# Two pairs of attention layers on one core: softmax sums, numerators, features and loads moved between engines, in a new written order

## The chip, the cores and the metric

The kernel runs on one core of a Trainium2 chip. The metric is the device time of one execution in microseconds. The kernel before took 480.94 us, the median of three runs (480.47 to 482.35). Engines are named as the profile names them: PE (TensorE), PEld (its weight loads), DVE (VectorE), ACT (ScalarE), POOL (GpSimd) and SP (SyncE, which here only issues transfers).

## The reference, cut to what matters

2,048 tokens of 512 features pass through a layer A, a layer B, and then both again with the same weights. Each layer is `x = x + layer(layernorm(x))`, with 32 heads of 16 features.

```python
# layer A, for each of 4 segments of 512 tokens
p = softmax(qs @ ks.T * scale + mask)              # causal, inside the segment
a_dot = p @ vs
a_mem = (phi(qs) @ M) / (phi(qs) @ z + 1e-6)       # phi(t) = t + 1 if t > 0 else exp(t)
o = g * a_mem + (1 - g) * a_dot                    # g = sigmoid(beta), one per head
M, z = M + phi(ks).T @ vs, z + phi(ks).sum()
# layer B, over all 2048 tokens
phi_k = concat(softmax(k @ w), softmax(-(k @ w)))  # 16 features each; phi_q alike
kv, z = phi_k.T @ v, phi_k.sum()
o = (phi_q @ kv) / (phi_q @ z + 1e-6)
# both: the heads are joined and multiplied by wo
```

## The kernel before

Tokens lie on the partitions in 16 tiles of 128; four tiles make a segment. The whole of `X` (bf16) and all weights stay in SBUF. Nothing loops at run time: `build` records every operation of the two pairs of layers in a graph, and `place` reads one order for all of them, the engine of each and the buffer of each tile from a packed table, `ORDER`. Each engine then runs its own list strictly in that order and waits on semaphores; a late instruction holds whatever stands behind it on its engine. PSUM is four tiles `D0` to `D3` of 128 x 1024 f32, shared by everything that PE writes.

The steps, by the functions that make them:

- `setup` loads inputs and weights on the queues of SP, ACT and POOL, and builds the gate from `beta`. The four token tiles of the first segment are loaded one by one, in turn on SP and ACT. `1 - g` is multiplied into layer A's value weights (four multiplications on POOL), `exp(beta)` into the mask `GAm` of the memory.
- `ln` normalises a tile: statistics, a root on POOL (on ACT for the first segment), and `xn` on DVE; with `flex` it may be on DVE or ACT.
- `a_proj` projects keys and queries of layer A into one PSUM tile. `Kev` and `Qev` copy the two halves to SBUF, `phi` reads the same PSUM half again for its exponential (`phexp`), and `Km` masks the keys per head into `KM`. Then come the values and the memory `M`.
- `a_att` is the causal attention: scores on PE, exponentials on ACT (`exp`, `expf`, `expd`, 1024, 896 and 768 elements per partition), weighted values on PE, the normalisation on DVE (`rden`, `pvn`). The sum of each softmax comes from a column of ones beside the values.
- `b_keys` takes four token tiles: exponentials of both signs on ACT, their sums over 16 features on DVE (`Zred`), reciprocals on DVE (`rZ`, line 389), values times reciprocals (`Vt`), and the product with the values, added up in `KV32`. After the last tile of a layer, `Rkv` and `Rz` are the masked results.
- `b_query` takes the four tiles of a segment: exponentials (`qexp`), sums (`Zq`, `zln`, `zs`), and for each tile a numerator `N` on PE. ACT copies it to SBUF in bf16 (`Nev`, line 351), DVE multiplies it by the weights (`nmul`, line 1043) and adds the two halves (`nadd`, line 1049). A DMA transpose or PE turns the result, and `out_proj` multiplies by `wo` and adds the residual.

Layer B's queries can begin when all keys of the layer are summed. In the order, the queries of the first layer B run beside the projections and the attention of the second layer A; the queries of the last layer B stand alone at the end.

Of the kernel before, what the change touches and what calls it, by code (L numbers as in the profile page):

```python
# [16 lines left out]
D = 512  # L17
H = 32
# [279 lines left out]
class Kernel:  # L298
# [151 lines left out]
    def setup(self):  # L450
# [19 lines left out]
        for t in range(4):  # L470
            ldx(t, 1, "act" if t % 2 else "sp")
        for h in range(2):
            for k in ("k", "q"):
                load(lambda k=k, h=h: [(self.WA[k][:, :, h * 256:(h + 1) * 256],
                                        inp["A_w" + k][:, h * 256:(h + 1) * 256].rearrange("(dt p) o -> p dt o", p=128))],
                     256, [R("WA", k, h)])
        load(lambda: [(self.beta_sb[:], inp["A_beta"].partition_broadcast(128))], 8, [R("beta")], "pool")
        load(lambda: [(self.wphi_st[:], inp["B_w_phi"].rearrange("(g hl) d j -> (hl d) g j", g=NG))], 60, [R("wphi")], "pool")
        ldw(lambda: self.WA["v"], inp["A_wv"], R("WA", "v"))
# [33 lines left out]
        for hf in range(2):  # L513
# [6 lines left out]
        self.act(lambda: gt[:, 0, :], lambda: self.beta_sb[:], ACT.Exp, 32, [R("beta")], [R("gt")], psum=False)  # L520
        v(lambda e: e.tensor_scalar(gt[:, 1, :], gt[:, 0, :], 1.0, None, op0=ALU.add), 100, [R("gt")], [R("gt1")])
        v(lambda e: e.reciprocal(gt[:, 2, :], gt[:, 1, :]), 270, [R("gt1")], [R("gt2")])
        v(lambda e: e.tensor_tensor(self.GAm[:, :, :, 0:16], gt[:, 0, :, None].to_broadcast([128, H, 16]).rearrange("p (g h) c -> p g h c", g=NG),
                                    self.H8[:, None, :, None].to_broadcast([128, NG, 8, 16]), ALU.mult), 620,
          [R("gt"), R("H8")], [R("GAm")], label="gates")
        v(lambda e: e.tensor_copy(self.GAm[:, :, :, 16], self.H8[:, None, :].to_broadcast([128, NG, 8])), 100,
          [R("H8")], [R("GAm")], label="gates")

        for dt in range(4):
            fn = lambda e, dt=dt: e.tensor_tensor(self.WA["v"][:, dt, :].rearrange("p (h d) -> p h d", h=H),  # L530
                                                  self.WA["v"][:, dt, :].rearrange("p (h d) -> p h d", h=H),
                                                  gt[:, 2, :, None].to_broadcast([128, H, DH]), ALU.mult)
            self.g.op({"dve": (602.0, fn), "pool": (1100.0, fn)}, [R("gt2"), R("WA", "v")], [R("WAv", dt)], label="gate")
# [95 lines left out]
    def phi(self, ps, dst, src=None, c=0):  # L629
# [28 lines left out]
    def a_proj(self, L, s):  # L658
# [7 lines left out]
        for g in range(NG):  # L666
# [11 lines left out]
            for sl in range(4):  # L678
# [3 lines left out]
                self.g.op({"dve": (262.0, fn)}, [KT, R("m4")], [KM[sl]], label="Km", port=True)  # L682
            st["KM"].append(KM)
            if pk:
                PK = self.T(self.p1, "PhK")
                self.phi(ps, pk, KT)
# [8 lines left out]
            if PQ:  # L695
                self.phi(ps, PQ, QT, 512)
                st["PhQ"].append(PQ)
        wv = lambda dt: self.WA["v"][:, dt, :].rearrange("p (k a e) -> p a k e", k=8, a=2)
        for t2 in (0, 2):
            ps = self.T(self.pD, "gen")  # L700
            self.tproj(ps, wv, [R("WAv", i) for i in range(4)], (t2, t2 + 1), lambda tt, dt: xT.t[:, dt, tt * 128:(tt + 1) * 128],
# [10 lines left out]
        if s < 3:  # L712
            for hp in range(2):
# [8 lines left out]
                if s == 0:  # L722
                    self.v(lambda e, pv=pv, g2=g2: e.tensor_copy(self.MS32[:, g2], pv()), 350, [ps[0]], [R("MS32", hp)], label="Macc")
# [178 lines left out]
    def kv_add(self, ps, q, first, last):  # L902
# [5 lines left out]
        if first:  # L908
            v(lambda e: e.tensor_copy(dst(), src()), 65 + 136 * n / 0.96, [ps[0]], [R("KV32", q)], label="KVacc")
# [12 lines left out]
    def b_keys(self, L, c, parts):  # L922
# [4 lines left out]
        for part in parts:  # L927
            Es, Vts = {}, {}
            units = [part[i:i + 2] for i in range(0, len(part), 2)]
            for u in units:  # L930
# [9 lines left out]
                for sgn in range(2):  # L940
# [46 lines left out]
    def b_query(self, L, c, store):  # L987
# [21 lines left out]
        zr = [ZQ[(gp, sgn)] for gp in range(2) for sgn in range(2)]  # L1009
        AB = self.T(self.pS, "AB")  # L1010
# [5 lines left out]
        self.act(lambda: u(0), lambda: zv(1, 1), ACT.Ln, 128, zr, [t1[0]], label="zln")  # L1016
# [41 lines left out]
    def build(self):  # L1058
# [5 lines left out]
        def lnA(L, s):  # L1064
            self.xA[(L, s)] = self.T(self.pX, "xA")
            for t in range(s * 4, s * 4 + 4):
                self.ln(t, self.xA[(L, s)], flex=(L == 1), pe=("xA", L, t) in PE_T, root="act" if L == 0 and s == 0 else "pool")

        for L in range(2):
            if L == 0:  # L1070
                lnA(0, 0)
                gate = self.xnop[3]
                for o in list(self.pV.init.values()) + list(self.pE.init.values()) + list(self.pF.init.values()):
                    o.deps.add(gate)
# [36 lines left out]
MASKED = {(0, 0)}  # L1111
N_XT, N_KM, N_K1, N_K2, N_VT, N_SM, N_QT, N_PE, N_PF = 5, 6, 16, 19, 5, 6, 6, 2, 3
PVW = 320
VSP = 1
VCOP = set()
# [7 lines left out]
COPIED = {(L, t) for L in range(2) for t in range(16)}  # L1123
# [6 lines left out]
c-rlH1Jo>AvgVG6?W~{2wr$(CZQHhO+qP}nwr!s?nRQOzzV~+bboadJS@YI<Syh?28DD%6Uu4x<m4sDhRakr$oh4>fSv6Lj)nGMQEmoV=VRczOR-ZLs4Ot`Bm^EQdS  # L1130
u@t0wO}n-E7qE|VQpDE)}D1>ahPUtSqv7F#bUsSAuGxpmX8%<FIaw7hFxO?SV2~tC1ZtHSyqmfXC)Y8oGB()5R1$#%g$c194sfx#Y(aYEH}H(Ua@HGHA}#5u$wGB%g
73|BCHfk&Pub2EDy`eDzX0T4okuAvPA3=OUNFxH|!p}&z`WSEE7x3(y(+aEz8QXu*}S`4D12B#X7P9tP>l^I<sM{AM3%Mu`x`tFzg`<W+Ci3i@*l4p=>Z4!n(7REFS
B^#<Fp2Jev$tU<#YfrotRH4Q8>ftQQ->y0M;Y8tcvGvK1^PRe*}Hh^=J(VF0XR17Qst1m&PStYzz1A2t+*v(;<~o5v=xg={2CMe|u-rZ6i_U<=r7_LfCqKDLi-VCz{
Vc90!lp)4#L1`>)vaVP|ZK|v8H3h&q`HWA)44WW>Vjb_<MV*oB@009sNCc$9X$TqPLY%?1I2wzzyC;_FR6qJFIP!{GwW|#*%U?)_Ds!$24z-Sl=W5B`}W*`g(0$>)X
21{9W$W7tkJ45`)rn1j$6wHRKFdg>59GC&wU@uI7nXnKR!7P}_Vzca!hX}T?PwX2D#NjXk#=|aH#&$z?%0bIn5QfF+EEo+EPG&(6g5l6&c;vVb7QlSigfo}}GueKq3
FBZZ+l;lKE^K3AAw5OF?QAS8hG19%KUia^4M|xB+QIfRAJl_{&;;s0bJ&21papEihR_I_LNjOytzZ>2fYs0jT0?yZU=dj$+s|r1C`QC=OkiS23n?HSBmoX>p&hh`43
G*A!6rDwj<LhA88$$AILwZ-l#mp5vy8A2mcbE-0L$Shtb>TK0@lMy=m2Y=BW!^akQy8m5DDTybchSlARfekn9vDwLR2O(9P?o;2oI4V4J?IIEC(<+f@|R@ZiNGIg6+
eDupdvtI_wFt;UtR>ogoTzfv9kV^@0R&lpVnBa2(d-L2Qfd@EB}^Q*auRL2t-NU7-(jgS?c9l0#qE$-2WX)*cUG2Rw{5u_yMzX4o9pU@hzc{oo9QKyBQ^*5WHnjMuO
wzQz`K9b01(Y=vF14X(mS*bT2>WK4>wFg>ouD3}4SVoZ#O@$nAy!QR*%??Mke3!SkqcEOI=4?E!&JO{Bb8pgn=7#q`IW{QI;Fgf<e0eBvg;WfAb*Wn&KfUUR#Ct@|+
iIZ>}4#n!Y9cy4dx&f)_CZwTTFc2@oFuZ}ga4+7%J$MuI!C1@>xA78OhLl(UcH=nA1>-R{49A3c1@b_2%!CgiBj$yiGyzB8WSoM7aR^Su(Kro{;TRl=CvX%V$5VI)Z  # L1140
^KoXjx#VnrN)_<mhQu2cm$d8EE|NgurB7J0(6?4#B+EDU%+X+i&yCyy@Xfr2F~JnEQ&AiB^JZtcmXeBTD*t%aW=leIhc;J&?UT#b?`M*#8NmHD`N?K3vclOK7of=1}
ot+{DhzJDSW`^_z|<<MY=>;F&jRIXHWnW;5#UUrLipL#Def13Sw@2g5U5vzQYgj9uLzI`Us!l6I`Y%^c4@%V|;|8=nFo@Lo|R!(?I$TBj^X@z#qsc50=A{$gnVG$0A
q-mtZbjid8WYj->r`fI8Aq8bqCl^J6ra1TRQqXe<??64aRr(>yFfJ*gL!q=__v`q41zPhS8z@vktBhSPBxO5^D?4WYc455ED>Bq~mmsWhFW6V!#y&?%DqI&~$*Z_s=
!MP;ZPmB*KKp3c!Ly25VL9qLV2*)m*?D{uiW#0zwn&eC4GM@WmX8118?M0Arl&7fN}lO7S{_vrymqlW}skdGeI6M9MkQ~`U?V$6?c*h)-?3urnurCHR67Se2bOU-Br
y`!bnm)cNsT1NA!5ze8x)EL`RJ8FW9XgR&6c@#>E={c>W6%>Zv&<hGnffPh7sXYagq$#9Glc80#nwp}eHDq~B^6^^a@Bkj3!chaNO%16mX>NEq8pH?lVE&PUcp#5J<
*5pNqN+5N)>3zRMsYEO99l>3=>vVH_4I`*Q3Z-bm8l|Cqlna)s?!FlK^tiZAId}c6#kul&{SRzr}6sujSBPWya@kFvv>pCPN6&uk4&ZcY+i;J<x!|SAI6LE3OqUu=V
# [83 lines left out]
```

## Time and profile before

| what | value |
|---|---|
| median of three runs | 480.94 us (480.47 to 482.35) |
| the profiled execution | 477.48 us |
| its span in the profile | 475.8 us |
| granted clock of PE, mean | 0.989 |
| read from memory, written | 6.32 MB, 2.10 MB |

The profile is of one execution, which was faster than the three timed ones. In the parts below, busy time is the time in which an engine had an instruction in its pipe; in a group's row stand the busy time of the group, the mean duration of one instruction in ns, and the idle time of the engine ahead of it with what ended it. Line 351 is the helper `act` and line 326 the helper `mm`, so rows there are told apart by tiles and shapes. `p`, `pS`, `pT`, `pX` are pools of SBUF buffers, `D` is PSUM.

### The profile page before, as it was taken

The page shows a single profiled execution, that of the slowest core. Times are in us where ns is not written, and L with a number is a line of the kernel's source. Part 1 is how long each engine was busy: PE and PEld are TensorE (multiplying, and loading weights), DVE is VectorE, ACT ScalarE, POOL GpSimd, SP SyncE. Part 2 cuts the span into 40 slices and gives each one's busy share as a digit, 9 for nine tenths or more (in the row PEclk, how much of TensorE's full clock was granted, in tenths as well). Part 3 has the DMA queues.
Part 4 walks back from the last instruction along what each step waited for, and adds up shares of the span by engine and source line. Part 5 has one row for each costly group of instructions (what it writes and reads, how often), then busy time and mean ns, then how long its engine had stood idle before and what let it go on. Part 6 is the DMA issues. An engine that isn't in the chain of part 4 may idle for free.

```text
span 475.8 us, 25262 instructions
## 1 busy us (share of the span) xinstructions
PE 451.6 (95%) x11582; PEld 299.1 (63%) x11582; DVE 435.3 (91%) x968; ACT 424.4 (89%) x560; POOL 61.0 (13%) x145
## 2 busy tenths in 40 slices
PE   8898999999999999998999999999999999999996
PEld 4356665757776676656556667576677666666553
DVE  6998999999899989988999999999999887998883
ACT  3598999999999997488999999999999999676892
POOL 4702020200011011100230031020011020110000
PEclk9999999999999999998999999999999999999799
DMA  8844353350243221200235544632105504100256
GB/s 228 210 111 96 65 88 48 61 92 4 60 83 48 26 37 26 41 2 4 47 68 82 73 73 48 98 60 38 25 4 81 61 15 69 28 12 3 47 100 193
DMA packets 89451, 30.37 MB, mean 64 GB/s; under 512 B 76000, under 2 KB 89344, under 8 KB 89344
## 3 DMA queue, kind: packets, MB, share of 16 engines
q1 hardware_dynamic: 88992, 28.46, 33.0%
q8 instruction: 91, 1.49, 1.3%
q10 hardware_dynamic: 288, 0.26, 0.2%
q0 software_dynamic: 64, 0.02, 0.2%
q14 instruction: 16, 0.13, 0.1%
HBM read 6.32 MB, written 2.10 MB: 18 GB/s over the span
## 4 chain that ended last, share of the span: by engine, by line
PE 62%; ACT 27%; DVE 5%; issue 2%; DMA 2%; SPq 1%; POOL 0%
PE D L341 39%; PE D L326 21%; ACT p L351 14%; ACT pF L351 8%; ACT pE L351 4%; PE D L649 2%; DVE pQ L679 1%; DMA pX<-p 1%; DMA p<-p 1%; SPq L364 1%; DVE p L1043 1%; DVE stats L577 1%; ACT pS L351 1%; PE D L378 1%; PE D L867 1%
## 5 line engine op out<-in xcount | busy, mean ns | idle before, releaser
L351 ACT ACTIVATE p<-D 128x1024 bf16<-128x1024 f32 (+1 forms) x276 | 251.5, 964 | 26.4 <-PE D L341 15.9
L351 ACT ACTIVATE pF<-D 128x896 bf16<-128x896 f32 x128 | 117.7, 942 | 2.1 <-PE D L326 1.7
L326 PE MATMUL D<-pK,pQ 64*128 64x256 bf16 (+3 forms) x1536 | 113.5, 243 | 5.8 <-DVE pQ L679 2.0
L326 PEld LDWEIGHTS D<-pK,pQ 64*128 64x128 bf16 x1536 | 55.3, 94 | 44.1 <-ACT p L351 6.7
L326 PE MATMUL D<-pV,pF 64*128 64x34 bf16 x1024 | 76.0, 176 | 1.8 <-ACT pE L351 0.5
L326 PE MATMUL D<-pW,pF 64*128 64x34 bf16 x1024 | 73.2, 176 | 0.3 <-issue 0.3
L341 PE MATMUL D<-pX,WA_k 64*128 64x512 bf16 x256 | 64.7, 376 | 0.8 <-DVE pX L360 0.7
L341 PE MATMUL D<-pX,WA_q 64*128 64x512 bf16 x256 | 64.7, 377 | 0.1
L585 POOL TENSOR_SCALAR rstd<-mv 128x1 f32<-128x1 f32 x60 | 16.5, 285 | 354.5 <-DVE mv L578 354.5
L326 PEld LDWEIGHTS D<-pV,pF 64*128 64x128 bf16 x1024 | 56.9, 93 | 4.3 <-issue 1.1
L326 PEld LDWEIGHTS D<-pW,pF 64*128 64x128 bf16 x1024 | 52.5, 93 | 1.6 <-issue 0.8
L351 ACT ACTIVATE pE<-D 128x768 bf16<-128x768 f32 x64 | 52.8, 835 | 0.2
L326 PE MATMUL D<-pV,p 64*128 64x34 bf16 x1024 | 52.1, 175 | 0.1
L326 PE MATMUL D<-pW,p 64*128 64x34 bf16 x1024 | 51.0, 176 | 0.0
L326 PEld LDWEIGHTS D<-pV,p 64*128 64x128 bf16 x1024 | 46.8, 93 | 2.5 <-ACT p L351 0.4
L326 PEld LDWEIGHTS D<-pW,p 64*128 64x128 bf16 x1024 | 45.1, 93 | 1.7
L326 PE MATMUL D<-tri,two 64*128 64x128 bf16 (+1 forms) x384 | 46.1, 234 | 0.0
L326 PE MATMUL D<-pV,pE 64*128 64x34 bf16 x512 | 45.2, 175 | 0.2 <-issue 0.2
L577 DVE BATCH_NORM_STATS2 stats<-X 128x6 f32<-128x512 bf16 x64 | 42.9, 681 | 1.5 <-DMA X<-in_A_x_dram 1.3
L679 DVE TENSOR_SCALAR pQ<-p,m 128x512 bf16<-128x512 bf16 x128 | 43.8, 363 | 0.0
L326 PE MATMUL D<-pW,pE 64*128 64x34 bf16 x512 | 42.6, 175 | 0.0
L945 DVE TENSOR_REDUCE pS<-p 128x64 f32<-128x1024 bf16 (+1 forms) x36 | 38.6, 1085 | 1.4 <-ACT p L351 1.3
(119 smaller groups left out, 1001.0 us busy)
## 6 DMA issues: line engine op xcount, KB each, us to landing
pW<-pV SPq DMA_DIRECT2D x16, 136.0 KB, 2.8
out_dram<-X SPq DMA_DIRECT2D x7, 256.0 KB, 2.8
X<-in_A_x_dram SPq DMA_DIRECT2D x3, 512.0 KB, 4.6
pX<-in_B_wqkv_dram SPq DMA_DIRECT2D x3, 512.0 KB, 4.9
p<-p SPq DMA_TRANSPOSE x76, 2.6
pX<-p SPq DMA_TRANSPOSE x54, 3.3
WA_k<-in_A_wk_dram SPq DMA_DIRECT2D x2, 256.0 KB, 6.7
WA_q<-in_A_wq_dram SPq DMA_DIRECT2D x2, 256.0 KB, 7.1
```

The costliest lines, as they stand in the source:

```text
L326: ins = e.matmul(out_ap, lhsT, rhs, start=st, stop=sp, tile_position=(basep(lhsT), basep(out_ap)))
L341: ins = e.matmul(out_ap, lhsT[64 * hf:64 * hf + 64], rhs[64 * hf:64 * hf + 64], start=k == 0 and i == 0, stop=k == 1 and i == len(lists[hf ...
L351: return self.g.op({"act": (dur, lambda e: e.activation(out_ap(), in_ap(), func, scale=scale))}, reads, writes, opens, label=label)
L364: return self.g.op({"sp": (1200.0, lambda e: [e.dma_start(out_ap(), in_ap(), transpose=True)])}, reads, writes, opens, kind="d", lat=1450. ...
L378: ins = e.transpose(pb()[:, k * 128:(k + 1) * 128], src()[:, k * 128:(k + 1) * 128], self.ident[:])
L577: v(lambda e: e.bn_stats(self.stats[:, t, :], self.X[:, t, :]), 602, [R("X", t)], [R("st", t)], label="bn")
L585: v(lambda e: e.tensor_scalar(rs, self.mv[:, t, 1:2], LN_EPS, None, op0=ALU.add), 170, [R("mv", t)], [R("rstd", t)], eng="pool", label="rstd")
L649: ins = e.matmul(D.t[c0:, r0 * 8:r0 * 8 + n], r[:, c0:], ones(r, n), start=True, stop=True, tile_position=(r0, c0))
L679: fn = lambda e, KM=KM, KT=KT, sl=sl: e.tensor_scalar(KM.t[:, :, sl % 2, :, 64 * (sl // 2):64 * (sl // 2) + 64], KT.t[:].rearrange("p (j h ...
L867: ins = e.matmul(tp.t[:, k * 128:(k + 1) * 128], pair.t[:, (k // 2) * 512 + sgn * 256 + (k % 2) * 128:(k // 2) * 512 + sgn * 256 + (k % 2) ...
L945: fn = lambda e, sgn=sgn, eo=eo, Z=Z, n=n: e.tensor_reduce(Z.t[:, 0:64 * n].rearrange("p (k s h) -> p k s h", k=n, s=2)[:, :, sgn, :], eo( ...
L1043: v(lambda e, Ns=Ns, Tm=Tm, w=w, shape=shape: e.tensor_tensor(shape(Tm.t[:]), shape(Ns.t[:]), w(), ALU.mult), 600, [Ns, AB[0], AB[1]], [Tm ...
```

## The change

It has six parts and a new table.

- Layer B's keys: where two tiles are taken together, the sums' reciprocals are made on ACT as exp(-ln(z)), one logarithm for the two tiles and one exponential for each, where DVE made them in one operation per tile.
- Layer B's queries: `COPIED` is empty, so `nmul` reads the numerator from PSUM and the copy `Nev` is gone.
- Layer A's features: `phi` reads the copied keys or queries from SBUF, and not the PSUM tile.
- The gate: `1 - g` is no longer multiplied into the value weights. The column beside the values holds `1 + exp(beta)` where it held ones, so that each softmax sum carries the gate; the mask of the memory changes to match. `beta` is loaded as one row and spread by a small matmul.
- Loads: the first segment comes in two loads of two tiles, one on ACT's queue and one on SP's; one half of the query weights moves to ACT's queue; `beta` moves from POOL's queue to SP's, and the load of `w_phi` waits for the fourth `xn`.
- Some operations may now be put on DVE or ACT (`xn` of two more segments, the first copies of `M` and `KV32`, `Km` in two segments), and the table decides.
- The table `ORDER` is new in whole: engine, place and buffer of each operation. In it five `xn` and four of the copies `ote` are on ACT that were on DVE, and no `Km` is.

```diff
-        for t in range(4):
-            ldx(t, 1, "act" if t % 2 else "sp")
+        ldx(0, 2, "act")
+        ldx(2, 2)
...
-                     256, [R("WA", k, h)])
-        load(lambda: [(self.beta_sb[:], inp["A_beta"].partition_broadcast(128))], 8, [R("beta")], "pool")
+                     256, [R("WA", k, h)], "act" if q else "sp")
...
+        load(lambda: [(self.beta_sb[0:1, :], inp["A_beta"][None, :])], 8, [R("beta0")])
...
-        for dt in range(4):
-            fn = lambda e, dt=dt: e.tensor_tensor(self.WA["v"][:, dt, :].rearrange("p (h d) -> p h d", h=H),
...
-            self.pV.init[i] = two(lambda e, tv=tv: e.memset(tv[:, :, :, 16:17], 1.0), 560.0, 190.0)
+            self.pV.init[i] = self.v(lambda e, tv=tv: e.tensor_copy(tv[:, :, :, 16:17], gt[:, 1, :][:, None, :, None].to_broadcast([128, 4, H, 1])), 200.0,
...
-        self.act(lambda: e_.t[:], lambda: ps.t[:, c:c + 512], ACT.Exp, 512, [ps[c]], [e_], label="phexp")
+        self.act(lambda: e_.t[:], lambda: src.t[:], ACT.Exp, 512, [src], [e_], psum=False, label="phexp")
...
+                Zr = [Z[0], Z[1]]
+                if n == 2:
+                    self.act(lambda Z=Z: Z.t[:, 0:128], lambda Z=Z: Z.t[:, 0:128], ACT.Ln, 128, Zr, Zr, psum=False, label="zkl")
                 for k, tt in enumerate(u):
                     Vt = Vts[tt] = self.T(self.pT, "Vt")
+                    if n == 2:
+                        self.act(lambda Vt=Vt: Vt.t[:, :, :, 16, :], lambda Z=Z, k=k: Z.t[:, k * 64:k * 64 + 64].rearrange("p (s g h) -> p s g h", s=2, g=NG), ACT.Exp, 64,
+                                 Zr, [Vt[("z", 0)], Vt[("z", 1)]], scale=-1.0, psum=False, label="zkl")
+                        continue
...
-                self.ln(t, self.xA[(L, s)], flex=(L == 1), pe=("xA", L, t) in PE_T, root="act" if L == 0 and s == 0 else "pool")
+                self.ln(t, self.xA[(L, s)], flex=(L == 1 or s < 2), pe=("xA", L, t) in PE_T, root="act" if L == 0 and s == 0 else "pool")
...
-COPIED = {(L, t) for L in range(2) for t in range(16)}
+COPIED = set()
...
```

More of the change, by code (lines that the diff above doesn't have):

```diff
@@ L700, in a_proj @@
             ps = self.T(self.pD, "gen")
[L701 removed]
+            self.tproj(ps, wv, [R("WA", "v")], (t2, t2 + 1), lambda tt, dt: xT.t[:, dt, tt * 128:(tt + 1) * 128],
                        [xT[t2], xT[t2 + 1]], opens=[VT] if t2 == 0 else [], label="V")
@@ L1009, in b_query @@
         zr = [ZQ[(gp, sgn)] for gp in range(2) for sgn in range(2)]
+        inps = (L, c) not in ZCOP
+        if not inps:
+            ZS = self.T(self.p2, "T")
+            two = lambda x: x.rearrange("p (a x) -> p a x", a=2)
+            self.evac(lambda: two(ZS.t[:].bitcast(F32)), lambda ZQ=ZQ: two(ZQ.t[:])[:, :, 0:256], 512, zr, [ZS], label="Zev")
+            zr = [ZS]
+            zv = lambda s, k: two(ZS.t[:].bitcast(F32)).rearrange("p a (s k x) -> p a s k x", s=2, k=2)[:, :, s, k, :]
         AB = self.T(self.pS, "AB")
@@ L1072, in build @@
                 gate = self.xnop[3]
+                self.loads[self.late].deps.add(gate)
                 for o in list(self.pV.init.values()) + list(self.pE.init.values()) + list(self.pF.init.values()):
@@ L1114 @@
 VSP = 1
+ZCOP = set()
 VCOP = set()
```

164 lines of the change are left out of this document (88 added, 76 removed).

## The prediction

> **What bounds the kernel now.** I read the page's busy lines first, then the busy time of each engine by stage, then the waits, then the groups of instructions of the whole run and of the last stage.
>
> ```profile
> PE 451.6 (95%) x11582; PEld 299.1 (63%) x11582; DVE 435.3 (91%) x968; ACT 424.4 (89%) x560; POOL 61.0 (13%) x145
> PE 62%; ACT 27%; DVE 5%; issue 2%; DMA 2%; SPq 1%; POOL 0%
> ```
>
> ```profile
> 0.00:11.40 11.40, 9.56 (x99) 4.83 (x100) 7.13 (x23) 4.26 (x12) 4.27 (x19) 1.00 0.88 224
> 40.00:185.00 145.00, 140.89 (x4191) 99.81 (x4189) 135.69 (x292) 141.92 (x179) 15.84 (x38) 1.00 0.32 53
> 185.00:214.84 29.84, 29.77 (x593) 18.93 (x587) 26.98 (x51) 19.84 (x24) 3.22 (x8) 1.00 0.09 18
> 214.84:260.00 45.16, 42.75 (x878) 25.51 (x872) 42.63 (x112) 43.58 (x67) 8.64 (x16) 0.96 0.30 53
> 260.00:400.00 140.00, 135.43 (x4046) 95.23 (x4044) 132.46 (x306) 137.55 (x176) 16.07 (x40) 1.00 0.36 53
> 400.00:438.85 38.85, 37.98 (x792) 24.01 (x788) 36.31 (x61) 28.37 (x34) 3.17 (x8) 1.00 0.09 19
> 438.85:475.80 36.95, 30.71 (x646) 17.61 (x644) 25.70 (x55) 26.40 (x43) 0.00 (x0) 0.90 0.45 110
> ```
>
> The columns are the stretch, its length, then busy PE, weight load, DVE, ACT and POOL. No engine has much room, and the tightest one changes. In the attention stretches (40 to 185 and 260 to 400) ACT is busy 97.9% and 98.2%; in the key stretches that end each layer's attention (185 to 214.84, 400 to 438.85) PE is (99.8%, 97.8%) and ACT has 10 us to spare; in the last stretch, layer 1's queries alone, all three have some room. The last wait of an attention stretch is PE held up by exponentials that have not yet read its PSUM tile:
>
> ```profile
> PEld D L326 <- ACT p L351: 10.6, 33, 0.9
> PEld D L326 <- ACT pF L351: 7.5, 28, 0.6
> ```
>
> **The change part by part.** Prices come from groups of the whole run (count | busy, mean ns):
>
> ```profile
> L1043 DVE TENSOR_TENSOR p<-p,pS 128x1024 bf16<-128x1024 bf16 x32 | 21.5, 686 | 2.0 <-ACT p L351 1.7
> L973 DVE TENSOR_TENSOR pT<-D,pT 128x1024 bf16<-128x1024 f32 x28 | 33.3, 1213 | 2.0 <-PE D L341 1.7
> L389 DVE RECIPROCAL pT<-pS 128x64 bf16<-128x64 f32 x28 | 14.4, 533 | 0.1
> L598 DVE TENSOR_SCALAR p<-X,mv,rstd 128x512 bf16<-128x512 bf16 x48 | 18.8, 402 | 0.9 <-POOL rstd L587 0.7
> L360 DVE CAST p<-D 128x512 bf16<-128x512 f32 x27 | 18.5, 685 | 2.2 <-PE D L867 1.7 <-PE D L341 0.4
> L351 ACT ACTIVATE p<-D 128x1024 bf16<-128x1024 f32 x220 | 222.5, 1049 | 23.9 <-PE D L341 14.5 <-PE D L326 7.7
> L351 ACT ACTIVATE p<-D 128x512 bf16<-128x512 f32 x56 | 32.9, 634 | 2.5 <-PE D L341 1.4 <-DVE p L360 1.0
> L351 ACT ACTIVATE pS<-pS 128x128 f32<-128x128 f32 x22 | 6.9, 326 | 0.2
> L351 ACT ACTIVATE pS<-D 128x128 f32<-128x128 f32 x8 | 2.3, 284 | 0.0
> L583 ACT ACTIVATE rstd<-rstd 128x1 f32<-128x1 f32 x4 | 0.7, 199 | 0.1
> L359 ACT ACTIVATE p<-D 128x512 bf16<-128x512 f32 x15 | 9.2, 611 | 5.5 <-PE D L341 5.2 <-PE D L867 0.4
> L592 DVE SCALAR_TENSOR_TENSOR nb<-mv,rstd 128x1 f32<-128x1 f32 x16 | 2.4, 152 | 0.3 <-POOL rstd L587 0.2
> ```
>
> Numerators from PSUM: 32 ACT copies of 128x1024 go, at 222.5/220 = 1.01 us that is 32.4 us of ACT. The 32 multiplications now read f32 from PSUM. That form is not in the trace; line 973 has the nearest (PSUM numerators times a broadcast bf16), 33.3/28 = 1.19 us against 21.5/32 = 0.67 for the SBUF form, so +0.52 each and +16.6 us of DVE. The low bound is 0.67 (no gain of width is lost), and nothing suggests above 1.22.
>
> Key sums on ACT: 28 reciprocals go, 14.4 us of DVE. In come 14 logarithms over 128 elements (0.31) and 28 exponentials over 64 that are not shown, between 0.20 (one element) and 0.33 (128); I take 0.27. That is 4.3 + 7.6 = 11.9 us of ACT (10 to 13.6). It also makes a chain DVE, ACT, DVE out of one that stayed on DVE.
>
> Features from SBUF: 48 exponentials over 512 read SBUF; rows of 128 elements differ by 326 - 284 = 42 ns, so +2.0 us of ACT (0 to 4). In return a projection's PSUM tile is free after one reader.
>
> Moved by the new order, counted from the built program: five normalisations of 0.40 us go from DVE to ACT (not shown there; some 0.65 by the 512-wide row, 3.2 us), eight small statistics of 0.15 us are added on DVE, and four transposed outputs go from DVE (0.69) to ACT (0.6). Sum for ACT: -32.4 + 11.9 + 2.0 + 3.2 + 2.4 and -0.6 for one value copy that leaves = -13.5 us. Sum for DVE: +16.6 - 14.4 - 2.0 + 1.2 - 2.7 + 0.7 + 0.4 of set-up = -0.2 us. PE's instructions stay but for one 32-column matmul. So the change is a trade, and what counts is where each half falls.
>
> Counting both programs' lists between the same events (last attention exponential, last key-value mask) at these prices gives, after minus before: attention of layer 0, ACT +4.8, DVE 0, PE +1.7; keys behind it, ACT -1.8, DVE -4.0, PE -4.2 (a query projection, four small sum products and half a value projection moved out); queries of layer 0 with attention of layer 1, ACT -2.2, DVE -1.1, PE +1.8; keys of layer 1, ACT -1.9, DVE -1.2, PE -0.9; the last stage, ACT -11.4, DVE +7.6, PE +1.7.
>
> Taken by the tightest engine of each stretch: +4 (ACT at 97.9%; 0 to +5), -4 (PE at 99.8%; -4.2 to 0), -1 (ACT; -5 to +2), -1 (PE; -1 to 0).
>
> The last stage has rows of its own:
>
> ```profile
> 437.56 1.28 DVE L915 TENSOR_TENSOR Rkv<-KV,H 128x512 bf16<-128x512 f32 x2
> 439.49 0.29 DVE L1018 TENSOR_TENSOR pS<-pS,D 128x128 f32<-128x128 f32 x1 [0.65 <-ACT pS L351]
> 439.81 0.29 DVE L1019 TENSOR_TENSOR pS<-pS,D 128x128 f32<-128x128 f32 x1
> 464.45 0.69 DVE L1043 TENSOR_TENSOR p<-p,pS 128x1024 bf16<-128x1024 bf16 x1 [0.51 <-ACT p L351]
> 470.10 1.22 DVE L898 TENSOR_TENSOR X<-X,D 128x1024 bf16<-128x1024 bf16 x1 [2.24 <-PE D L341]
> 471.44 0.60 ACT L359 ACTIVATE X<-D 128x512 bf16<-128x512 f32 x1 [1.79 <-PE D L341]
> L1049 DVE TENSOR_TENSOR p<-p 128x512 bf16<-128x512 bf16 x14 | 5.8, 421 | 0.2
> L898 DVE TENSOR_TENSOR X<-X,D 128x1024 bf16<-128x1024 bf16 x4 | 4.8, 1216 | 2.4 <-PE D L341 2.2
> ```
>
> Before, DVE's last numerator ends at 464.45 + 0.69 = 465.14, 26.3 us after the masks (437.56 + 1.28 = 438.84). In the new list DVE does, between those two events, 20 small sums at the 0.32 that lies between starts here (6.4), 16 multiplications of 1.19 (19.0), 13 additions of 0.41 (5.4) and a residual of 1.2: 32.0 us, to which come the 0.65 before the first and about 1 us of other gaps. The last numerator then ends near 33.6, 7.3 later. Of the 475.8 - 465.14 = 10.7 us behind it some 2.3 come back: two of its three residual additions of 1.2 us now lie before it, and the rest (transpose, copy, projection, evacuation, store) hangs on the last tile as before. So the stage costs +5 (+2 to +8): it is bound by DVE, and ACT's freed 11 us stand idle there.
>
> The start: two tokens' tiles per load, one load on each queue, and a weight half on ACT's queue.
>
> ```profile
> X<-in_A_x_dram ACTq DMA_DIRECT2D x2, 128.0 KB, 2.8
> X<-in_A_x_dram SPq DMA_DIRECT2D x2, 128.0 KB, 4.4
> WA_q<-in_A_wq_dram SPq DMA_DIRECT2D x2, 256.0 KB, 7.1
> 2.29 0.44 SPq L457 DMA_DIRECT2D WA_k<-in_A_wk_dram  x1
> 6.66 0.29 ACT L581 ACTIVATE rstd<-mv,epsln 128x1 f32<-128x1 f32 x1 [3.67 <-DVE mv L578]
> 11.40 0.37 PE L341 MATMUL D<-pX,WA_k 64*128 64x512 bf16 x1 [0.72 <-DVE pX L360]
> ```
>
> The same 128 KB landed in 2.8 us from ACT's queue and 4.4 from SP's with its backlog, so the load that leads to PE's first projection at 11.40 could come 1 us sooner. Against that the query weights are now issued behind ACT's first root (6.66 + 0.29) and, at 2.8 to 7.1 us, land at 9.8 to 14. The gate's load leaves POOL's queue for SP's, ahead of the key weights: one issue, 0.44 us. The load that stays on POOL now waits for the fourth normalisation; behind it stand only roots of later tiles. I count 0 (-1 to +3). The Trainium skill's page "DMA: Bandwidth & Descriptors", section "Issuing engines are not separate DMA queues", says that loads from several engines share the same 16 DMA engines and save only issue time; the rows above show a gain beyond that, and by the page the start would be no better than 0.
>
> The gate in the sums' column takes four weight multiplications off POOL (busy 13%) and nothing off the path; their cover is that the value projection comes later.
>
> Sum: 0 + 4 - 4 - 1 - 1 + 5 = +3 us. The profiled execution took 477.48 us, 475.8 of it span; it becomes 480.5. The runs' median of 480.94 lies 3.46 above the profiled one, so the forecast is 484.0.
>
> **The rivals.** (1) Faster. Projections free their PSUM tile after one reader, and ACT's copies are gone from the queries of layer 0, where ACT is busy 43.58 of 45.16 us. If the 18 us of weight loads held up by exponentials shrink by a quarter, the attention terms become +2 and -5 instead of +4 and -1, the start -1 and the tail, with DVE's gaps filled, +3: -1 + 2 - 4 - 5 - 1 + 3 = -6, 478. It decides once ACT's stalls there fall by over 3 us. Against it: ACT's work before the last stage falls by 1 us only. (2) Slower by a new wait: ACT's logarithm of the key sums waits for DVE's reduction with the exponentials of attention queued behind it. The crossing ACT to DVE cost 0.65 at 439.49; 14 crossings there, on an ACT that has no slack, are 9 us, of which I let half stand: 488.5. For it: DVE is busy 93% and more of the attention stretches, so its reductions can run late. It decides if the reductions come less than 0.65 before their logarithm. (3) No change to be told: the trade evens out, 481. (4) The tail's clock. The last stage was granted 0.90; with DVE as its bound PE has longer gaps. At 0.5 its 30.71 busy us would be 55, 13 more than the some 42 us of my tail: 497. The Trainium skill's "TensorE: Matmul & The Clock Gate", section "HAM oscillation — how this bites in real kernels", says that PE gaps above about 3.4 us halve the clock; no gap so long shows in the rows here.
>
> **How the numbers follow.** Forecast 0.40, rival 1 0.25, rival 2 0.15, rival 3 0.17, rival 4 0.03. What can be told from no change here is 0.5%, 2.4 us. The forecast's own range is 479 to 490, since the bounds of its terms do not all fall on one side; a tenth of the total lies in it within 2.4 us and 0.03 below. Faster: 0.22 of rival 1 and 0.03, 0.25. Same: 0.10, 0.03 of rival 1, 0.15 of rival 3: 0.28. Slower: the rest, 0.47. The range is 476 to 490: it leaves out the far half of rival 1, rival 4 and part of rival 2.
>
> **What would show it.** Right: numerators near 1.2 us each; DVE busy about 33 us behind the last mask with ACT below 18, that stage some 42 us long, and the key stretch of layer 0 shorter by 4 while its attention is longer by as much. Wrong: a tail no longer than 38 us, numerators under 1 us, or an attention stretch that shrinks. Rival 2 would show as ACT waiting for DVE's reduction in the waits.

## The result: 2.3 us longer, and the profile after

| | median | range | ratio to before |
|---|---|---|---|
| before | 481.29 us | 479.13 to 485.20 (20 runs) | 1 |
| after | 483.63 us | 479.83 to 489.26 (20 runs) | 1.0048 (95%: 1.0025 to 1.0071) |

The changed kernel is 2.3 us longer, 1.2 to 3.4 by the interval: told apart from zero, and about half a per cent. One run of after, 489.26 us, fell in a slower state and is left out of the ratio. The forecast was 484.0. The profiled execution of after took 479.83 us, the shortest of its twenty, with 478.0 us of span against 475.8 before; its stages therefore show 2.2 us of the difference, and its start, as will be seen, is luckier than most.

The page after, busy time and the chain that ended last:

```profile
PE 453.6 (95%) x11583; PEld 296.6 (62%) x11583; DVE 433.1 (91%) x944; ACT 410.4 (86%) x578; POOL 51.6 (11%) x138
PE 58%; ACT 18%; DVE 18%; DMA 4%; issue 2%; POOL 1%; SPq 0%; DVEq 0%
```

ACT lost 14.0 us (forecast 13.5) and DVE 2.2 (forecast 0.2). The chain moved from ACT (27% to 18%) to DVE (5% to 18%) and PE stayed its largest part.

The same chain of stages, cut at the same events in both kernels (first projection, last attention exponential of layer 0, its last key-value mask, the two for layer 1, the end). Columns as in the prediction. Before:

```profile
0.00:11.40 11.40, 9.56 (x99) 4.83 (x100) 7.13 (x23) 4.26 (x12) 4.27 (x19) 1.00 0.88 224
11.40:185.84 174.44, 166.28 (x4604) 113.65 (x4606) 164.90 (x364) 165.19 (x210) 25.58 (x56) 1.00 0.39 73
185.84:214.76 28.92, 28.85 (x538) 18.21 (x536) 26.16 (x50) 18.93 (x24) 3.22 (x8) 1.00 0.09 18
214.76:408.13 193.37, 186.39 (x5151) 126.23 (x5145) 181.58 (x426) 189.02 (x252) 25.40 (x58) 0.99 0.34 52
408.13:438.84 30.71, 29.84 (x576) 18.60 (x568) 29.81 (x52) 20.55 (x24) 2.49 (x7) 1.00 0.07 15
438.84:475.80 36.96, 30.72 (x646) 17.61 (x644) 25.71 (x56) 26.41 (x43) 0.00 (x0) 0.90 0.45 110
```

After, with the part of the last stage up to the last numerator as a row more:

```profile
0.00:11.91 11.91, 10.12 (x99) 4.88 (x100) 6.59 (x26) 4.81 (x13) 1.75 (x14) 1.00 0.90 248
11.91:185.10 173.19, 166.33 (x4606) 112.76 (x4608) 160.81 (x363) 167.32 (x225) 20.69 (x53) 1.00 0.42 71
185.10:212.42 27.32, 27.13 (x514) 17.07 (x512) 24.64 (x47) 17.79 (x27) 3.22 (x8) 1.00 0.09 17
212.42:407.43 195.01, 188.27 (x5172) 126.15 (x5166) 180.19 (x411) 185.27 (x257) 22.76 (x57) 1.00 0.32 52
407.43:437.34 29.91, 29.28 (x580) 18.30 (x573) 28.70 (x47) 19.80 (x31) 3.13 (x8) 1.00 0.07 15
437.34:478.00 40.66, 32.43 (x654) 17.41 (x646) 32.21 (x54) 15.37 (x29) 0.00 (x0) 0.90 0.47 100
437.34:468.20 30.86, 27.01 (x586) 14.30 (x580) 28.74 (x52) 13.57 (x26) 0.00 (x0) 0.89 0.39 58
```

| stage | forecast | after less before in the two profiles |
|---|---|---|
| start | 0 | +0.5 |
| attention of layer 0 | +4 | -1.2 |
| keys of layer 0 | -4 | -1.6 |
| queries of layer 0, attention of layer 1 | -1 | +1.6 |
| keys of layer 1 | -1 | -0.8 |
| last stage | +5 | +3.7 |
| sum | +3 | +2.2 |

The last stage is the only large term, and DVE, 25.7 us busy there before, has 32.2 now while ACT falls from 26.4 to 15.4. A single profile moves by itself, though: the last mask of layer 1 ended between 437.3 and 442.4 us in the profiles of after, a_load4, hybrid, a_tail_quick and a_l0_quick, which differ little ahead of it. So the terms of 1 or 2 us need the runs below.

The last stage itself is steadier. From the last mask to the end it took 36.96, 36.93, 36.55 and 36.35 us in the four profiles of kernels that have before's last stage unaltered (before, b_act_load, b_phi_sbuf, b_zk_act), and 40.66, 39.73, 39.88 and 39.81 us in the four that have after's (after, a_rz_dve, a_load4, a_l0_quick): 3.3 us more on average. In the second four the granted clock of the stage was 0.90, 0.98, 0.93 and 0.93: at 0.98 the stage was 0.1 us shorter than at 0.93, so it is not PE's clock that sets its length.

The groups that carry the prices, after:

```profile
L1068 DVE TENSOR_TENSOR p<-D,pS 128x1024 bf16<-128x1024 f32 x32 | 38.3, 1218 | 1.6 <-PE D L326 1.4
L351 ACT ACTIVATE pT<-pS 128x64 bf16<-128x64 f32 x28 | 6.6, 266 | 0.1
L351 ACT ACTIVATE p<-pK 128x512 bf16<-128x512 bf16 x24 | 15.1, 640 | 0.0
L351 ACT ACTIVATE p<-p 128x512 bf16<-128x512 bf16 x24 | 14.9, 636 | 0.1
L598 ACT ACTIVATE p<-X,nb,rstd 128x512 bf16<-128x512 bf16 x5 | 3.9, 809 | 0.3 <-DVE nb L595 0.2
```

A numerator from PSUM took 38.3/32 = 1.20 us (1.19 in the sum), a key exponential 0.27 (as estimated), the features 15.1 + 14.9 + 4.7 for the eight that still read PSUM = 34.7 against 32.9 (+1.8; 2.0 in the sum), a normalisation on ACT 0.8 (0.65 in the sum). The prices were near, though the features' came out by another way: their instructions were no longer than before (640 and 636 ns against a mean of 634), so the 42 ns more for each did not show, and only the busy time rose. What the prices did to the time was not right, stage by stage.

### The profile page after: what moved, and what is told of

Its sections match the earlier page's. It is cut to its first block, busy times and chain, and to the rows that moved or that the text cites. A ratio compares the mean times of both kernels' runs of the same rounds, so it can differ in the third digit from the quotient of the medians.

```text
span 478.0 us, 25222 instructions
## 1 busy us (share of the span) xinstructions
PE 453.6 (95%) x11583; PEld 296.6 (62%) x11583; DVE 433.1 (91%) x944; ACT 410.4 (86%) x578; POOL 51.6 (11%) x138
## 4 chain that ended last, share of the span: by engine, by line
PE 58%; ACT 18%; DVE 18%; DMA 4%; issue 2%; POOL 1%; SPq 0%; DVEq 0%
PE D L341 38%; PE D L326 18%; ACT pF L351 7%; ACT p L351 7%; ACT pE L351 3%; DVE stats L580 3%; DVE p L1068 2%; DMA p<-p 2%; PE D L652 2%; DVE X L906 1%; DVE pQ L682 1%; DMA pX<-p 1%; DVE pV L360 1%; DVE p L360 1%; DVE pK L360 1%
## 5 line engine op out<-in xcount | busy, mean ns | idle before, releaser
L351 ACT ACTIVATE p<-D 128x1024 bf16<-128x1024 f32 (+1 forms) x196 | 194.3, 1016 | 11.9 <-PE D L341 8.9
L326 PE MATMUL D<-pK,pQ 64*128 64x256 bf16 (+3 forms) x1536 | 114.8, 243 | 4.9 <-ACT pF L351 2.1
L351 ACT ACTIVATE pF<-D 128x896 bf16<-128x896 f32 x128 | 115.6, 928 | 2.8 <-PE D L326 2.1
L588 POOL TENSOR_SCALAR rstd<-mv 128x1 f32<-128x1 f32 x60 | 14.4, 248 | 362.2 <-DVE mv L581 357.9
L682 DVE TENSOR_SCALAR pQ<-p,m 128x512 bf16<-128x512 bf16 x128 | 42.0, 348 | 0.9 <-ACT p L359 0.8
L1068 DVE TENSOR_TENSOR p<-D,pS 128x1024 bf16<-128x1024 f32 x32 | 38.3, 1218 | 1.6 <-PE D L326 1.4
```

The costliest lines, as they stand in the source:

```text
L326: ins = e.matmul(out_ap, lhsT, rhs, start=st, stop=sp, tile_position=(basep(lhsT), basep(out_ap)))
L351: return self.g.op({"act": (dur, lambda e: e.activation(out_ap(), in_ap(), func, scale=scale))}, reads, writes, opens, label=label)
L588: v(lambda e: e.tensor_scalar(rs, self.mv[:, t, 1:2], LN_EPS, None, op0=ALU.add), 170, [R("mv", t)], [R("rstd", t)], eng="pool", label="rstd")
L682: fn = lambda e, KM=KM, KT=KT, sl=sl: e.tensor_scalar(KM.t[:, :, sl % 2, :, 64 * (sl // 2):64 * (sl // 2) + 64], KT.t[:].rearrange("p (j h ...
L1068: v(lambda e, N=N, Tm=Tm, w=w, shape=shape: e.tensor_tensor(shape(Tm.t[:]), shape(N.t[:]), w(), ALU.mult), 1131, [N, AB[0], AB[1]], [Tm], ...
```

## The experiments

Every kernel was timed in five rounds beside the kernel before on its own chip. Differences are made between ratios, since chips differ by some tenths of a microsecond. "After" is the changed kernel. Where an operation was added or taken out, the other operations keep their place in the order unless it is said.

### The numerators in the last stage

**Quick numerators after** (label a_tail_quick) keeps every wait and the order and makes the last layer's 16 multiplications cheap.

```diff
-  e.tensor_tensor(shape(Tm.t[:]), shape(N.t[:]), w(), ALU.mult)
+  e.tensor_tensor(shape(Tm.t[:]), shape(self.WB["q"][:, 0:2, :].rearrange("p a b -> p (a b)") if L == 1 else N.t[:]), w(), ALU.mult)
```

> The changed kernel, its order and its waits untouched; in the last layer's queries the 16 multiplications take a bf16 weight tile in SBUF in place of the numerators in PSUM (the numerators of that layer are left out of the result). Only their duration changes, 1.19 to 0.67 us. Theory (DVE binds the last stage): the stage falls from 40.7 us by 4 to 7, the time to 477 to 480. Rival (PE, or the order of that stage, binds it): less than 2 us. The two kernels run before in which the copies were moved by hand do not decide this, since they also moved PE's and ACT's work.

Measured: 480.56 us, ratio 0.9989 (0.9955 to 1.0023), that is 2.8 us less than after (0.9 to 4.8). Groups and waits of this run:

```profile
L1068 DVE TENSOR_TENSOR p<-WB_q,pS 128x1024 bf16<-128x1024 bf16 x16 | 10.8, 688 | 6.2 <-PE D L326 6.2
L1068 DVE TENSOR_TENSOR p<-D,pS 128x1024 bf16<-128x1024 f32 x16 | 19.2, 1218 | 0.2
```
```profile
DVE p L1068 <- PE D L326: 6.2, 6, 2.4
```

The upper row is the last layer's, the lower layer 0's. DVE's work fell by 19.2 - 10.8 = 8.4 us and the time by 2.8: the cheap numerators now wait 6.2 us for PE to make the next one (1.4 us in after). So DVE is the bound of the changed tail, but PE stands only 1 to 3 us behind it. In this run's profile the stage took 38.76 us, 1.3 less than the mean of the four above and 1.9 less than after's own: short of the 4 to 7 expected, and inside the rival's 2. The dear numerators are then a part of the tail's 3.3 us. What holds the stage 2 us above before's 36.7 once they are cheap, PE or the new order, was not tried.

**Heavy numerators before** (b_tail_heavy) is the mirror image: the last layer's multiplications of the kernel before read f32 from SBUF, copies and order untouched.

```diff
-  e.tensor_tensor(shape(Tm.t[:]), shape(Ns.t[:]), w(), ALU.mult)
+  e.tensor_tensor(shape(Tm.t[:]), shape(Ns.t[:] if L == 0 else self.KV32[:].rearrange("p a b -> p (a b)")[:, 0:1024]), w(), ALU.mult)
```

> The kernel before, its order, copies and waits untouched; in the last layer's queries the 16 multiplications take f32 from SBUF (the key-value sums, so that layer's numerators are left out), which should last 1.1 to 1.2 us in place of 0.67. Theory (that stage of the kernel before is close to bound by DVE, too): +4 to +8 us, 485 to 489. Rival (ACT's copies bind it, DVE has room): below +2.

Measured: 485.85 us, ratio 1.0095 (1.0061 to 1.0129), 4.6 us more than before.

```profile
L1043 DVE TENSOR_TENSOR p<-KV,pS 128x1024 bf16<-128x1024 f32 x16 | 19.2, 1219 | 0.1
L1043 DVE TENSOR_TENSOR p<-p,pS 128x1024 bf16<-128x1024 bf16 x16 | 10.8, 684 | 0.9 <-ACT p L351 0.9
```

The same 8.4 us of DVE cost 4.6 us here, as expected, in an order that has the copies in it; the stage took 42.5 us in the profile, 5.8 above the mean of before's four. Together: the dearer numerator alone, with nothing else changed, makes the run 3 to 5 us longer, and the stage in the profiles 1 to 2 in the new order and 6 in the old.

**Quick numerators of layer 0** (a_l0_quick): the same edit with `L == 0`.

> The same for the queries of the first layer B, which run beside attention: its 16 multiplications take a bf16 weight tile in SBUF (that layer's numerators are left out), 1.19 to 0.67 us, order and waits untouched. Theory (the longer multiplication cost 1 to 3 us there, where the stretch grew by 1.6 us against the kernel before although ACT had less to do): 1 to 4 us faster than the changed kernel. Rival (DVE has room there): within 1 us.

Measured: 482.72 us, ratio 1.0026 (0.9991 to 1.0061), 1.1 us less than after, which its interval doesn't tell from nothing and which lies between the theory and the rival. Beside attention the same 8.4 us of DVE are mostly hidden.

**The old tail on the new kernel** (hybrid): after up to the last layer's masks, then the order, engines and copies of before (the table `ORDER` changes too and is not shown).

```diff
-COPIED = set()
+COPIED = {(1, t) for t in range(16)}
```

> The changed kernel up to its last key-value mask, and from there on the order, the engines and the ACT copies of the kernel before (182 operations). Theory (the change is 1 to 1.5 us quicker up to that mask, and gives back 3.7 us in the last stage): 437.3 + 37.0 = 474.3 us of span against 475.8 of the kernel before and 478.0 of the changed one, so 479 to 480, better than both by little. Rival (the two parts do not fit together, or the first part's gain was chance between two profiles): 481 or more.

Measured: 480.66 us, ratio 0.9990 (0.9968 to 1.0013): 2.8 us less than after (1.3 to 4.3), the same as before, and a little above the 479 to 480 expected. By the runs that is the whole loss, put back by the last stage alone. The profile bears out less of it: the stage took 38.5 us, not the expected 37.0 (39.1 in hybrid_load4 below). The two orders do not meet well there. The first small sum starts 2.2 us behind the last mask, where before's started 0.65 behind it, because two query exponentials (2.08 us on ACT, from 439.85) still run then, which in before had begun 2 us ahead of the mask's end (at 436.87).

**Two misses.** a_copy_tail puts the 16 copies back into after's own tail order, each behind its numerator; b_psum_tail takes them out of before's.

```diff
# a_copy_tail, on after
-COPIED = set()
+COPIED = {(1, t) for t in range(16)}
# b_psum_tail, on before
-COPIED = {(L, t) for L in range(2) for t in range(16)}
+COPIED = {(0, t) for t in range(16)}
```

> The changed kernel with the 16 copies to SBUF on ACT put back for the queries of the last layer alone, each right behind its numerator. Theory (the last stage is bound by DVE, which multiplies from PSUM at 1.19 us): DVE's 16 multiplications fall to 0.67 each, DVE is busy 24 us behind the last mask in place of 32, the stage goes from 40.7 us to 36.5 to 37.5, and the time is 3 to 4 us below the changed kernel's 483.6, so 480. Rival (the stage is bound by PE at a granted clock of 0.9, or by the chain zln, zs, numerator): the stage stays within 1.5 us of 40.7.

> The kernel before with the numerators of the last layer's queries multiplied straight from PSUM: 16 copies on ACT gone, nothing else changed but that PE's writes into a PSUM tile wait for DVE. Theory: the last stage grows from 37.0 us by 4 to 7 (this order was not made for it), 485 to 488. Rival (the new order is what costs, not the multiplication from PSUM): within 1.5 us of 481.3.

Measured: 493.98 us, ratio 1.0286 (1.0252 to 1.0319), and 494.32, ratio 1.0277 (1.0239 to 1.0314). Both half-changes cost 11 to 13 us, each far more than the whole change. A numerator in a_copy_tail's timeline, and waits of b_psum_tail:

```profile
474.92 0.69 DVE L1065 TENSOR_TENSOR p<-p,pS 128x1024 bf16<-128x1024 bf16 x1 [3.71 <-ACT p L351]
```
```profile
ACT p L351 <- PE D L341: 30.8, 12, 9.5
PEld D L326 <- DVE p L1046: 9.4, 5, 3.7
DVE p L1046 <- PE D L326: 5.8, 6, 2.2
```

With the copies DVE waits for them, 3.71 us at the longest; without them PE waits for DVE to read a numerator's PSUM tile, and ACT waits 30.8 us for PE where it waited 15.9 before. Neither tells what a numerator costs: they tell what an order costs that was written for other operations. That is why the runs above change a duration and leave the order.

### The key sums' reciprocals

**Back on DVE in the new order** (a_rz_dve):

```diff
-                Zr = [Z[0], Z[1]]
-                if n == 2:
-                    self.act(..., ACT.Ln, 128, Zr, Zr, psum=False, label="zkl")
...
-                    if n == 2:
-                        self.act(..., ACT.Exp, 64, ..., scale=-1.0, psum=False, label="zkl")
-                        continue
```

> The changed kernel with the key sums' reciprocals on DVE again (28 reciprocals of 0.51 us in place of 42 small ACT instructions), each where its exponential stood in the order. Theory (attention is bound by ACT as much as by DVE, so the trade of 14.4 us of DVE for 11.9 us of ACT is near to nothing): within 2 us of the changed kernel. Rival A (the reciprocals on ACT hold up the exponentials of attention): faster by 3 to 6 us. Rival B (DVE is what binds the attention of the new order): slower by 4 to 10 us.

Measured: 488.39 us, ratio 1.0157 (1.0125 to 1.0189), 5.2 us more than after (3.4 to 7.1), which is rival B's size: 10 us more of DVE (443.1 us busy against 433.1) cost half of that. The order was made for reciprocals on ACT, though, so this run too holds the price of an order written for other operations.

**On ACT in the old order** (b_zk_act): the same edit the other way, on before, each new ACT operation put where the DVE operation had stood.

> The kernel before with the key sums' reciprocals on ACT: the logarithm right behind the second reduction, each exponential where the reciprocal stood. All else and the order as before. Theory (an even trade): within 2 us of the kernel before. Rival A (ACT has no slack there, and waits for DVE's reductions): 4 to 12 us slower, with ACT waiting for the reductions in the waits. Rival B (DVE gets the slack that it lacked): 2 to 5 us faster.

Measured: 506.79 us, ratio 1.0542 (1.0508 to 1.0575): 26 us more than before, the sign and the waits of rival A and over twice its size. Its waits and two of its groups:

```profile
ACT pS L351 <- DVE pS L945: 16.7, 6, 3.8
PEld D L326 <- ACT p L351: 15.3, 33, 3.5
PEld D L326 <- ACT pF L351: 14.8, 25, 4.6
DVE pT L980 <- ACT pT L351: 8.1, 5, 2.4
```
```profile
L351 ACT ACTIVATE pS<-pS 128x128 f32<-128x128 f32 x36 | 11.3, 323 | 16.9 <-DVE pS L945 16.7
L351 ACT ACTIVATE pT<-pS 128x64 bf16<-128x64 f32 x28 | 6.3, 258 | 0.3
```

Line 945 is the reduction `Zred`. The logarithm waits 16.7 us for it, PE's weight loads behind the attention's exponentials wait 30.1 us where they waited 18.1, and DVE waits 8.1 us for the exponential to come back. This is the mechanism of the prediction's rival 2, in the old order.

**The load without the wait** (b_act_load): before, with 56 free-standing exponentials on ACT at those same places.

```diff
+                for k in range(4 if n == 2 else 0):
+                    self.act(lambda q=self.nscr: self.scr[:, q:q + 2], lambda: self.onesb[:, 0:2], ACT.Exp, 2, [R("onesb")], ...)
```

> The kernel before, with 56 free-standing small exponentials (two elements each, some 0.2 us by the 0.199 us of a one-element ACT row, 11 to 12 us in all) on ACT at the places where the key sums' chain stood in the run that moved the reciprocals to ACT in the old order; they wait for nothing and nobody waits for them, and the reciprocals stay on DVE. That run cost 26 us. Theory (the 26 us came from the chain, DVE to ACT and back, with the attention's exponentials queued behind a waiting logarithm): the same work without the wait costs little more than ACT's own busy time in the stretches where ACT has no slack, 4 to 12 us, so 485 to 493. Rival (the 26 us came from ACT being overfull, the waits being only how that shows): most of it returns, 500 or more.

Measured: 481.99 us, ratio 1.0032 (1.0003 to 1.0061): 1.5 us.

```profile
L351 ACT ACTIVATE scr<-onesb 128x2 bf16<-128x2 bf16 x56 | 8.2, 218 | 0.0
```
```profile
PE 453.8 (94%) x11582; PEld 299.8 (62%) x11582; DVE 435.9 (91%) x968; ACT 429.1 (89%) x616; POOL 60.8 (13%) x145
```

They kept ACT busy for 8.2 us by their row, against 6.3 and some 4.4 (14/36 of 11.3) for the chain. Even if 1.5 is scaled up by that, it gives 2 us of the 26: what is left, by elimination, is the waiting. And 1.5 is below the 4 to 12 that was expected of the load alone. Multiplied out, the row is 56 x 0.218 = 12.2 us; as busy time it is 8.2, ACT's whole busy time rose by 4.7 (424.4 to 429.1), and the run by 1.5: such short instructions overlap with their neighbours, and what they add is mostly absorbed.

In the new order the same chain waits for little, 1.8 us for the reduction and 1.6 for the exponential to come back. Waits of after:

```profile
PEld D L326 <- ACT pF L351: 8.6, 25, 0.8
PEld D L326 <- ACT p L351: 6.8, 22, 1.1
ACT pS L351 <- DVE pS L953: 1.8, 3, 1.1
DVE pT L988 <- ACT pT L351: 1.6, 1, 1.6
```

### The features and the start

**Features from SBUF alone** (b_phi_sbuf), on before:

```diff
-        self.act(lambda: e_.t[:], lambda: ps.t[:, c:c + 512], ACT.Exp, 512, [ps[c]], [e_], label="phexp")
+        self.act(lambda: e_.t[:], lambda: src.t[:], ACT.Exp, 512, [src], [e_], psum=False, label="phexp")
```

> The kernel before with one part alone: the 48 exponentials of the features read the copied keys and queries from SBUF and not PSUM, in the old order and with the same copies. Theory (the step costs ACT some 2 us at 42 ns each and adds the copy ahead of each exponential, while projections come at places where their PSUM tile is not short): 0 to +3 us, 480.5 to 484. Rival (freeing a projection's PSUM tile after one reader shortens PE's 18 us of weight loads held up by exponentials): faster by 1 to 4 us, 476.5 to 479.5.

Measured: 481.83 us, ratio 1.0015 (0.9983 to 1.0047). No gain of the size that rival 1 needs, and PE's weight loads wait as long as before:

```profile
PEld D L326 <- ACT p L351: 10.5, 31, 1.0
PEld D L326 <- ACT pF L351: 7.7, 27, 0.6
```

**Single loads** (a_load4 on after, hybrid_load4 on the hybrid): the four token tiles come one by one again; the query weights stay on ACT's queue.

```diff
-        ldx(0, 2, "act")
-        ldx(2, 2)
+        for t in range(4):
+            ldx(t, 1, "act" if t % 2 else "sp")
```

> The changed kernel with the four token tiles loaded one by one again, all else as in the changed kernel. Theory: first statistics near 3.7 instead of 4.5 us, and 0.5 to 1.5 us less than the changed kernel (483.6), so 482 to 483. Rival (query weights on ACT's queue set the first query projection, so the token tiles do not matter): no difference, 483.6.

> The changed kernel up to the last layer's masks, the last stage as in the kernel before, and the four token tiles of the first segment loaded one by one again, in turn on two queues. Theory (the paired loads brought the first statistics 0.8 us later and the start 0.5 us): 0.5 to 1.5 us below the run with the paired loads, so 479 to 480, the fastest of all. Rival (attention, not the loads, sets the time after the start): the same time, within 0.5 us.

Measured: 481.49 us, ratio 1.0018 (0.9992 to 1.0045), and 479.62 us, ratio 0.9972 (0.9945 to 0.9999). Each is some 1 us below its partner (1.4 and 0.9); taken together 1.2, with an interval that reaches to zero. The second is the fastest kernel of the study, though only 1.35 us below before. First statistics, a_load4 and then after:

```profile
3.64 0.69 DVE L580 BATCH_NORM_STATS2 stats<-X 128x6 f32<-128x512 bf16 x1 [2.58 <-DMA X<-in_A_x_dram]
```
```profile
4.46 1.29 DVE L580 BATCH_NORM_STATS2 stats<-X 128x6 f32<-128x512 bf16 x2 [3.39 <-DMA X<-in_A_x_dram]
```

So the paired loads bring the first tile 0.8 us later. The first projection, though, waits for something else: the query weights on ACT's queue, which are issued together with ACT's first root and so behind those statistics. Their issue, their time from issue to landing and the first projection in after, and then the first projection of a_load4, a_rz_dve and hybrid_load4:

```profile
5.86 0.42 ACTq L457 DMA_DIRECT2D WA_q<-in_A_wq_dram  x1
WA_q<-in_A_wq_dram ACTq DMA_DIRECT2D x1, 256.0 KB, 6.0
11.91 0.37 PE L341 MATMUL D<-pX,WA_k 64*128 64x512 bf16 x1 [0.68 <-DVE mv L581]
```
```profile
11.15 0.37 PE L341 MATMUL D<-pX,WA_k 64*128 64x512 bf16 x1 [0.17 <-DMA WA_q<-in_A_wq_dram]
```
```profile
14.04 0.58 PE L341 MATMUL D<-pX,WA_k 64*128 64x512 bf16 x1 [3.54 <-DMA WA_q<-in_A_wq_dram]
```
```profile
12.85 0.37 PE L341 MATMUL D<-pX,WA_k 64*128 64x512 bf16 x1 [0.76 <-DMA WA_q<-in_A_wq_dram]
```

In after 5.86 + 6.0 = 11.86, just ahead of 11.91, though its row names a statistic. In all eight profiles with a weight half on ACT's queue the sum of issue and landing time comes within 0.2 us before the first projection. The landing time was 6.0 to 8.2 us; the issue was at 5.80 to 5.92 us with the paired loads and at 4.59 and 4.71 with the single ones. So single loads help by bringing that issue 1.1 to 1.3 us forward, and the spread of the landing hides it in a single profile (11.15 and 12.85).

In the six profiles of kernels with the paired loads it started at 11.91, 12.76, 14.04, 12.66, 14.23 and 12.09 us, a mean of 12.95, and in five of them the row names the query weights. In the six with the old loads it was 11.40, 12.54, 11.67, 11.65, 11.80 and 12.07, a mean of 11.86, and one names them. The start costs some 1.1 us, and more than 2 in some executions; the profiled execution of after is the best of its six. That all of it reaches the end of the run is not shown.

## Why the prediction was right, and where its steps were not

The sign, and the last stage as the main term, held: 483.6 measured, 484.0 forecast. That the total came within 0.4 us is luck. In the two profiles the stages missed their forecasts by +0.5, -5.2, +2.4, +2.6, +0.2 and -1.3, 12.2 us in all without regard to sign, and these happen to cancel to -0.8. One of the prediction's own signs of being wrong came true, an attention stretch that shrinks. And 2.3 us lies inside the 2.4 that it counted as no change, so rival 3 was near; only the twenty runs of each tell the two apart.

By the runs the difference is made of about +2.8 in the last stage (hybrid, a_tail_quick; 3.3 by the stage in four profiles each), +1.1 at the start (first projections of twelve profiles) and what is left, 2.3 - 2.8 - 1.1 = -1.6, in attention and keys. That remainder carries the spread of all three, 1 to 2 us. The old tail and old-style token loads on the changed kernel, 1.35 us below before, give nearly the same.

- **The last stage: mechanism right, size over.** Numerators of 1.2 us, DVE busy 32.2 us (some 33 forecast), ACT 15.4 (under 18), a stage of 40.7 (some 42). It cost 3.7 us in the two profiles (3.3 in four each) and 2.8 in the runs, not 5. That DVE binds the stage is shown in part: quick numerators give back 1 to 3 us before PE takes over. The mis-sized term is DVE's sum of 32.0 us up to the last numerator: by the row of the stretch DVE was busy 28.74 of 30.86 us. The durations held, but an instruction that waits for nothing starts some 0.08 us before the one ahead of it ends, as the starts and durations of DVE's timeline after show (463.91 to 464.25 with 0.43, 464.25 to 465.38 with 1.21, 466.63 to 466.98 with 0.42):

```profile
463.91 0.43 DVE L1071 TENSOR_TENSOR p<-p 128x512 bf16<-128x512 bf16 x1
464.25 1.21 DVE L906 TENSOR_TENSOR X<-X,D 128x1024 bf16<-128x1024 bf16 x1
465.38 1.22 DVE L1068 TENSOR_TENSOR p<-D,pS 128x1024 bf16<-128x1024 f32 x1
466.63 0.42 DVE L1071 TENSOR_TENSOR p<-p 128x512 bf16<-128x512 bf16 x1
466.98 1.22 DVE L1068 TENSOR_TENSOR p<-D,pS 128x1024 bf16<-128x1024 f32 x1
468.11 2.34 DVE L906 TENSOR_TENSOR X<-X,D 128x1024 bf16<-128x1024 bf16 x2
471.86 1.22 DVE L906 TENSOR_TENSOR X<-X,D 128x1024 bf16<-128x1024 bf16 x1 [1.40 <-PE D L341]
```

  Against that, the 2.3 us that were to come back behind the last numerator were 0.9 (10.66 to 9.80): three residual additions still lie behind it, two at 468.11 and one at 471.86, as in before (465.52, two, and 470.10). The prediction said that two of them would lie ahead of it, while its own sum of 32.0 us holds only one, the one that stood ahead in before as well (452.95).

- **Attention of layer 0: wrong, +4 against -1.2.** The step that failed took ACT's share (97.9% between 40 and 185 us) for a bound on which each added microsecond falls due. ACT's busy time rose by 2.1 us (165.19 to 167.32, with 15 instructions more) where 4.8 were counted, and the stretch became shorter. b_act_load shows both without the rest of the change: small activations fill less of ACT than their durations add up to, and the run grows by less than that again.
- **Keys of layer 0: sign right, -1.6 against -4.** PE's busy time there fell by 1.7 us and not by the 4.2 counted, and in the attention ahead of it PE's work didn't rise by the 1.7 counted (166.33 after 166.28). The two lists had been cut at operations of ACT and DVE. The likely reason, which no run tests, is that PE works ahead of those, so that a place in a list is not a place in time.
- **Queries of layer 0 with attention of layer 1: sign wrong, +1.6 against -1.** The term was taken by ACT, whose work did fall (by 3.8 us), but PE's rose by 1.9, as counted, and the stretch followed PE. That rests on two profiles; b_act_load and b_phi_sbuf only support that ACT isn't the bound.
- **The start: 0 against about +1.** The condition was in the text: query weights "behind ACT's first root" that land at 9.8 to 14 us. They landed 11.9 to 14.1 us into the run in the six profiles with paired loads and set the first projection in each; the value taken between -1 and +3 was too hopeful. The Trainium skill's page "DMA: Bandwidth & Descriptors", section "Issuing engines are not separate DMA queues", has it that loads from several engines share the same DMA engines, so that a second queue saves only issue time. The measured starts agree with it: none of the six was earlier than before's 11.40.
- **Rival 1 (faster)** needed PE's waits for exponentials to fall by over 3 us; they fell from 18.1 to 15.4, just short of that, and the tail stayed dear. The rival's time was added up wrongly: its -6 us from 480.94 is 475, not 478, and so below the stated range. **Rival 2 (the logarithm's wait)** is real and large in the old order (26 us, of which 1.5 to 2 is load); in the new one the logarithm waits 1.8 us. The new order is what hides it; how much of that comes from an earlier reduction and how much from other moves wasn't tried. **Rival 4** didn't occur: the last stage was granted 0.90 before and after.

The gate in the sums' column and the operations that changed engine besides were not tried one by one. Outside the last stage they lie in the remainder of -1.6 us.

## What to carry to other kernels

Where each engine runs a list written out in advance, an operation and its place are one thing: the same reciprocals on ACT cost 26 us in one order and, in the other, spare 5 us against DVE. To price one instruction there, make it cheaper or dearer and leave the list alone. Work taken off an engine is worth what that engine bounds in the stage where it falls: half of the copies left a stage where ACT had 10 us to spare, and what replaced them landed on the engine that had to finish it.

## What the runs showed of the hardware that was not expected

- The width of the operand set the price of a numerator, not where it lay: f32 from SBUF took 1.219 us, f32 from PSUM 1.218, bf16 from SBUF 0.684 to 0.688 (bf16 in PSUM wasn't tried).
- Durations of short instructions don't add up: 56 activations of 0.218 us raised ACT's busy time by 4.7 us and the run by 1.5, and DVE's instructions in the last stage that wait for nothing overlap the one ahead by some 0.08 us each.
- The same load of 256 KB of weights, issued on the same queue at 5.80 to 5.92 us, took 6.0 to 8.2 us to land in six profiles and let the first projection start anywhere from 11.9 to 14.2 us.
